# Attention inputs packed into one array, and its products as 64 by 64 tiles

## The chip, the core and the metric

The kernel runs on one core of one Trainium2 chip. The metric is the device time of one execution in microseconds (us); the lower the better. Each core has five engines with a queue of instructions each: PE (TensorE, matrix products), DVE (VectorE), ACT (ScalarE), POOL (GpSimd) and SP (SyncE), whose queue here issues nearly all of the transfers (DMAs) between memory and the core. Engines wait for one another, and for transfers, through semaphores.

## What is computed

The reference chains three layers over 4608 tokens of width 512:

```python
# 1: attention within chunks of 64 tokens, 8 heads of 64
scores = scale * np.matmul(q_c, k_c.transpose(0, 1, 2, 4, 3))
scores = scores - np.max(scores, axis=-1, keepdims=True)
attn = np.exp(scores)
attn = attn / (np.sum(attn, axis=-1, keepdims=True) + 1e-09)
out = np.matmul(attn, v_c)
# 2: a mixture of 8 experts, each token to its best one, or to none where x @ w_skip <= 0
h = np.maximum(xc[mask] @ w1[e], 0.0)
y[mask] = gate_w[mask, None] * (h @ w2[e])
# 3: a gated linear unit
g = x @ w_gate
silu = g * (1.0 / (1.0 + np.exp(-g)))
return (silu * (x @ w_val) @ w_out)
```

Only the first layer's input and its two products (scores, and attention times values) are touched by the change; everything is float32 there.

## The kernel before

The program has three stages: attention with the routing of tokens to experts, the experts, and the gated linear unit. The order of the instructions on each engine is written out by hand. The change lies in the first stage.

**Tiles.** The attention stage loops over 36 tiles `i` of 128 tokens, that is of two chunks of 64 tokens with 8 heads. Heads are held in pairs: partitions 0 to 63 hold the first head of each of four pairs, partitions 64 to 127 the second. A step of the loop does, in this order: `qk(i)` (scores of tile i on PE into the PSUM tile `s`), `pv(i-2)` (values, PE into `o`), for one tile in four a piece of the routing, `sums(i-1)` (DVE), `ta(i-1)` (four transposes on PE into `at`, copied to `ats` by ACT), `tx(i-4)` (the store of a finished tile `x` to the array X in memory, four transposes into `xp`, a copy by ACT), then `soft(i)` (DVE: the maximum `mx`, and `a`, scores minus maximum), `norm(i-2)` (DVE: `x`, `o` divided by the sums) and `expo(i)` (ACT). Small DVE instructions of the routing are threaded in between, one after each DVE step (`link`).

**Routing.** For each group of four tiles there are `route_a` (PE products `lp`, copied by ACT), `route_b` (PE transposes `lt`, then a chain of small DVE steps that begins with `L`), and `route_c` (small PE products `rp`, more DVE steps up to `slots`). When `slots` of a group is there, POOL scatters the group's tokens into the table `perm` by four indirect DMAs (L707).

**Inputs.** Queries, keys and values are three arrays in memory. One load serves a group `g` of two tiles (256 tokens): `load_qk` issues the queries of 512 KB over 128 partitions (L498), and the keys in two DMAs of 256 KB, each over 64 partitions (L501); `load_v` does the same with the values (L506). Keys and values go into zero-padded buffers, `kbd` and `vbd`, three of each: the first head's half stands in the columns of `h2` = 0 with zeros in the other partitions, the second head's half in those of `h2` = 1. So one product of 128 rows, 64 columns of the array and 128 streamed columns (2 heads by 64) gives both heads of a pair for one chunk: eight for `qk`, eight for `pv`. The profile has two matmul records for each float32 product, 16 for each call. From tile 3 on, every odd tile issues the load of the group that lies two after its own.

**Weights.** From tile 16 on each step also splits a slice of an expert's weights (`pump`): a DMA of 512 KB into `st` for every second tile, ACT and POOL work on it.

PSUM has eight banks: `s` two buffers of one bank, `o` two buffers of one bank, `at`, `xp`, `lp` and the routing's `m` one bank each.

The functions that the change touches, with the line numbers of the profile:

Of the kernel before, what the change touches and what calls it, by code (L numbers as in the profile page):

```python
# [31 lines left out]
NG = NT // GT  # L32
NTILE = NT // P
RT = 4
# [15 lines left out]
def attention_moe_glu_kernel(  # L50
    ctx: ExitStack,
    tc: tile.TileContext,
    qT: bass.AP,
    kT: bass.AP,
    vg: bass.AP,
# [229 lines left out]
    # the first 256 tokens are among the first 256 of their experts: no further tile holds one  # L285
# [146 lines left out]
    ctx.enter_context(tc.manual_schedule())  # L432
    with ExitStack() as actx:
        lctx = ExitStack()
        ld = lctx.enter_context(tc.tile_pool(name="ld", bufs=1, side="right"))
        ldq = actx.enter_context(tc.tile_pool(name="ldq", bufs=3))
# [3 lines left out]
        ps_s = actx.enter_context(tc.tile_pool(name="ps_s", bufs=2, space=PSUM))  # L440
        ps_a = actx.enter_context(tc.tile_pool(name="ps_a", bufs=1, space=PSUM))
        ps_m = actx.enter_context(tc.tile_pool(name="ps_m", bufs=1, space=PSUM))

# [8 lines left out]
        # the tensor engine's clock rises with work: keep it busy while it has to wait  # L452
# [15 lines left out]
        # the first unit of the first expert takes tokens of the first groups only  # L468
# [10 lines left out]
        NB = 3  # L479
        kbd = [ld.tile([P, 2, HP, GT], F32, name=f"kbd{i}") for i in range(NB)]  # L480
        vbd = [ld.tile([P, 2, GT // CH, HP, D], F32, name=f"vbd{i}") for i in range(NB)]
        for i in range(NB):
            nc.gpsimd.memset(kbd[i][0:64, 1], 0.0)
            nc.gpsimd.memset(kbd[i][64:128, 0], 0.0)
            nc.gpsimd.memset(vbd[i][0:64, 1], 0.0)
            nc.gpsimd.memset(vbd[i][64:128, 0], 0.0)
# [5 lines left out]
        def load_qk(g, parts=1):  # L492
            t = ldq.tile([P, HP, GT], F32, tag="q", name="q")
            q_t[g] = t
            n = GT // parts
            for o in range(parts):
                sl = slice(o * n, (o + 1) * n)
                nc.sync.dma_start(out=t[:, :, sl], in_=qT[:, g, :, sl])  # L498
                for h2 in range(2):
                    r = slice(64 * h2, 64 * h2 + 64)  # L500
                    nc.sync.dma_start(out=kbd[g % NB][r, h2, :, sl], in_=kT[r, g, :, sl])  # L501

        def load_v(g):
            for h2 in range(2):
                r = slice(64 * h2, 64 * h2 + 64)
                nc.sync.dma_start(out=vbd[g % NB][r, h2], in_=vg[r, g])  # L506
# [30 lines left out]
        def qk(i):  # L537
            g, o = divmod(i, 2)
            s = ps_s.tile([P, H, CH], F32, tag="s", name="s")
# [9 lines left out]
            s_t[i] = s  # L549

        def soft(i):
            s = s_t.pop(i)
            mx = sp.tile([P, H], F32, tag="mx", name="mx")
# [588 lines left out]
```

## Time and profile before

| | |
|---|---|
| median of 3 runs | 1407.55 us (1405.59 to 1407.98) |
| span of the profiled execution, first to last instruction | 1403.8 us |
| attention loop: first score product to last `a` | 5.73 to 168.94 us |
| first product of the experts (`hp`) | 180.14 us |
| PE busy over the span | 1334.5 us (95%) |
| DVE, ACT, POOL busy | 711.4, 451.3, 287.1 us |

The profiled execution has its span alone, no time of its own as the runs have it: the median of the runs is 3.75 us longer than the span. Times in the rows are microseconds from the first instruction. PE busy is high in all stages, also where PE waits between products for little at a time, so the stage is read from the waits and from the steps of the loop.

### The profile page before, as it was taken

The page shows a single profiled execution, that of the slowest core. Times are in us where ns is not written, and L with a number is a line of the kernel's source. Part 1 is how long each engine was busy: PE and PEld are TensorE (multiplying, and loading weights), DVE is VectorE, ACT ScalarE, POOL GpSimd, SP SyncE. Part 2 cuts the span into 40 slices and gives each one's busy share as a digit, 9 for nine tenths or more (in the row PEclk, how much of TensorE's full clock was granted, in tenths as well). Part 3 has the DMA queues.
Part 4 walks back from the last instruction along what each step waited for, and adds up shares of the span by engine and source line. Part 5 has one row for each costly group of instructions (what it writes and reads, how often), then busy time and mean ns, then how long its engine had stood idle before and what let it go on. Part 6 is the DMA issues. An engine that isn't in the chain of part 4 may idle for free.

```text
span 1403.8 us, 21388 instructions
## 1 busy us (share of the span) xinstructions
PE 1334.5 (95%) x8357; PEld 1209.5 (86%) x8357; DVE 711.4 (51%) x1301; ACT 451.3 (32%) x891; POOL 287.1 (20%) x245
## 2 busy tenths in 40 slices
PE   7877889998999999999999999999999999999998
PEld 6766678887788788899999999999999999999998
DVE  6856757888887788533232333333233333232322
ACT  2434535666665533312121221212121122121221
POOL 3134544564655366300000000000000000000000
PEclk9989999999999999999999999999999999999999
DMA  9999847887787744110202020100101020201000
GB/s 231 274 247 265 225 134 231 264 298 263 266 298 244 232 152 151 35 38 1 46 0 46 1 46 0 39 8 28 18 5 42 0 46 0 46 1 39 0 23 16
DMA packets 136713, 150.86 MB, mean 107 GB/s; under 512 B 79744, under 2 KB 82304, under 8 KB 136610
## 3 DMA queue, kind: packets, MB, share of 16 engines
q1 hardware_dynamic: 131778, 138.82, 34.7%
q0 software_dynamic: 4832, 10.65, 2.2%
q8 instruction: 66, 1.08, 0.3%
q14 instruction: 37, 0.30, 0.1%
HBM read 125.61 MB, written 25.28 MB: 107 GB/s over the span
## 4 chain that ended last, share of the span: by engine, by line
PE 72%; DMA 13%; DVE 6%; issue 4%; ACT 2%; POOL 2%; SPq 0%; another core or an unknown queue 0%; ACTq 0%; POOLq 0%; DVEq 0%
DMA kbd<-in_kT_dram 8%; PE o L250 7%; PE o L249 7%; PE o L248 7%; PE pg L250 6%; PE pg L248 6%; PE pg L249 6%; PE pv L248 6%; PE pv L250 6%; PE pv L249 6%; DVE wlo L148 2%; DMA st<-in_moe_w_dram 2%; DMA perm<-pair,slots 2%; PE y L250 2%; PE hp L249 1%
## 5 line engine op out<-in xcount | busy, mean ns | idle before, releaser
L1081 DVE TENSOR_TENSOR sg<-pg,sg 128x384 f32<-128x384 f32 (+1 forms) x132 | 72.1, 546 | 326.7 <-ACT sg L1080 326.7
L1085 ACT ACTIVATE uh<-sg 128x384 fp32r<-128x384 f32 (+1 forms) x156 | 78.1, 501 | 312.0 <-DVE sg L1082 312.0
L250 PE MATMUL pg<-xh,glo 128*128 128x384 f32 (+1 forms) x528 | 175.5, 332 | 0.0
L248 PE MATMUL pg<-xh,ghi 128*128 128x384 f32 (+1 forms) x528 | 175.1, 332 | 0.0
L249 PE MATMUL pg<-xl,ghi 128*128 128x384 f32 (+1 forms) x528 | 174.8, 331 | 0.0
L248 PE MATMUL pv<-xh,ghi 128*128 128x384 f32 (+1 forms) x528 | 173.9, 329 | 0.0
L249 PE MATMUL pv<-xl,ghi 128*128 128x384 f32 (+1 forms) x528 | 173.9, 329 | 0.0
L250 PE MATMUL pv<-xh,glo 128*128 128x384 f32 (+1 forms) x528 | 173.9, 329 | 0.0
L250 PE MATMUL o<-ghi,ul 128*128 128x512 f32 x432 | 171.1, 396 | 2.2 <-POOL ul L1087 2.2
L248 PE MATMUL o<-ghi,uh 128*128 128x512 f32 x432 | 168.7, 391 | 2.6 <-ACT uh L1085 2.6
L249 PE MATMUL o<-glo,uh 128*128 128x512 f32 x432 | 170.6, 395 | 0.0
L1080 ACT ACTIVATE sg<-pg 128x384 f32<-128x384 f32 (+1 forms) x132 | 63.6, 482 | 312.6 <-PE pg L250 312.6
L148 DVE TENSOR_TENSOR wlo<-st,whi 128x512 fp32r<-128x512 f32 x165 | 145.0, 913 | 14.5 <-ACT whi L146 13.2
L146 ACT ACTIVATE whi<-st 128x512 fp32r<-128x512 f32 x240 | 138.2, 625 | 34.6 <-DMA st<-in_moe_w_dram 30.9
L1082 DVE TENSOR_TENSOR sg<-pv,sg 128x384 f32<-128x384 f32 (+1 forms) x132 | 72.1, 546 | 118.6 <-PE pv L250 118.5
L148 POOL TENSOR_TENSOR wlo<-st,whi 128x512 fp32r<-128x512 f32 x75 | 101.4, 1353 | 127.6 <-ACT whi L146 116.9
L1087 DVE TENSOR_TENSOR ul<-sg,uh 128x384 fp32r<-128x384 f32 (+1 forms) x132 | 72.2, 547 | 76.8 <-ACT uh L1085 76.8
L248 PEld LDWEIGHTS pg<-xh,ghi 128*128 128x128 f32 x528 | 99.4, 188 | 5.9
L249 PEld LDWEIGHTS pg<-xl,ghi 128*128 128x128 f32 x528 | 99.3, 188 | 5.7
L250 PEld LDWEIGHTS o<-ghi,ul 128*128 128x128 f32 x432 | 81.0, 188 | 21.7 <-POOL ul L1087 4.4
L250 PEld LDWEIGHTS pv<-xh,glo 128*128 128x128 f32 x528 | 99.3, 188 | 0.0
L249 PEld LDWEIGHTS pv<-xl,ghi 128*128 128x128 f32 x528 | 99.3, 188 | 0.0
(164 smaller groups left out, 2525.2 us busy)
## 6 DMA issues: line engine op xcount, KB each, us to landing
st<-in_moe_w_dram SPq DMA_DIRECT2D x120, 512.0 KB
vbd<-in_vg_dram SPq DMA_DIRECT2D x36, 256.0 KB
X<-x SPq DMA_DIRECT2D x36, 256.0 KB
out_dram<-os SPq DMA_DIRECT2D x36, 256.0 KB
q<-in_qT_dram SPq DMA_DIRECT2D x17, 512.0 KB
kbd<-in_kT_dram SPq DMA_DIRECT2D x34, 256.0 KB
xr<-X SPq DMA_DIRECT2D x128, 64.0 KB
gst<-in_moe_w_gate_dram SPq DMA_DIRECT2D x12, 512.0 KB
```

The source lines that it names most:

```text
L146: nc.scalar.activation(out=hi[:, k, :], in_=stage[:, k % 2, :], func=ACTF.Copy)
L148: eng.tensor_tensor(out=lo[:, k, :], in0=stage[:, k % 2, :], in1=hi[:, k, :].bitcast(F32), op=ALU.subtract)
L248: nc.tensor.matmul(ps, ah, bh, start=start, stop=False)
L249: nc.tensor.matmul(ps, ah, bl, start=False, stop=False)
L250: nc.tensor.matmul(ps, al, bh, start=False, stop=stop)
L1080: nc.scalar.activation(out=u, in_=pg, func=ACTF.Sigmoid)
L1081: nc.vector.tensor_tensor(out=u, in0=pg, in1=u, op=ALU.mult)
L1082: nc.vector.tensor_tensor(out=u, in0=pv_, in1=u, op=ALU.mult)
L1085: nc.scalar.activation(out=uh, in_=u, func=ACTF.Copy)
L1087: eng.tensor_tensor(out=ul, in0=u, in1=uh.bitcast(F32), op=ALU.subtract)
```

## The change

It does five things.

- The three arrays become one, `qkv`, in which each partition holds for each tile the queries, keys and values one after the other. `load` brings two tiles (256 tokens) with one DMA of 1536 KB over 128 partitions, 12 KB in a row in each; the first two tiles come in three DMAs. There are four buffers (`NB`), and tile i issues the load of tiles i+5 and i+6.
- `kbd`, `vbd`, their zero fills on POOL and the two DMAs by halves are gone.
- `qk` and `pv` become sixteen products each, of 64 rows by 64 columns by 64 streamed columns. A product of the first head of a pair uses partitions 0 to 63, one of the second head 64 to 127.
- The two heads' results go to different PSUM banks, so `s` and `o` take two banks each and have one buffer each. DVE reads `s` and `o`, and writes `a` and `x`, with the heads in that order (`by_half`).
- `tx` always uses the one buffer `xp`; before, the last four tiles had used the buffers of `s`. After the loop the four banks go to a pool `ps_u`. A tile of its own, `x0`, replaces a query buffer that the first gather of the experts had used.

```diff
+        def load(i, parts=1):
+            if parts == 2:
...
+                nc.sync.dma_start(out=t[:, 0, 0:2], in_=qkv[:, i, 0:2])
+                nc.sync.dma_start(out=t[:, 0, 2], in_=qkv[:, i, 2])
+                nc.sync.dma_start(out=t[:, 1], in_=qkv[:, i + 1])
+            else:
+                t = ld.tile([P, 2, 3, HP, P], F32, tag="q", name="q")
+                nc.sync.dma_start(out=t, in_=qkv[:, i:i + 2])
...
+        def quads():
             for hp in range(HP):
                 for c in range(2):
-                    t0 = o * P + c * CH
-                    nc.tensor.matmul(
-                        s[c * 64:c * 64 + 64, 2 * hp:2 * hp + 2, :],
-                        q_t[g][:, hp, t0:t0 + CH],
-                        kbd[g % NB][:, :, hp, t0:t0 + CH],
-                        start=True, stop=True,
-                    )
+                    for h2 in range(2):
+                        yield hp, slice(64 * c, 64 * c + 64), h2, slice(64 * h2, 64 * h2 + 64)
+
+        def qk(i):
+            t = q_t[i]
+            s = ps_s.tile([P, 2, 2 * HP, CH], F32, tag="s", name="s")[:, :, 0:HP, :]
+            for hp, c, h2, r in quads():
+                nc.tensor.matmul(s[c, h2, hp, :], t[r, 0, hp, c], t[r, 1, hp, c], start=True, stop=True)
             s_t[i] = s
...
+            ps = ps_s.tile([P, 2, 2 * HP, D], F32, tag="o", name="o")[:, :, 0:HP, :]
+            for n, (hp, c, h2, r) in enumerate(quads()):
+                d = (n // 2 % 2) * HP + hp
+                nc.tensor.matmul(
+                    ps[c, h2, hp, :], t[r, hp, c], v[r, 2, d // 2, (d % 2) * D:(d % 2) * D + D],
+                    start=True, stop=True,
+                )
...
-            if i < NTILE - LAG:
-                p = ps_a.tile([P, KD, P], F32, tag="xp", name="xp")
-            else:
-                p = ps_s.tile([P, KD, P], F32, tag="s", name="xp")
+            p = ps_a.tile([P, KD, P], F32, tag="xp", name="xp")
...
-            if i % 2 == 1 and 3 <= i < NTILE - 4:
-                load_qk(i // 2 + 2)
-                load_v(i // 2 + 2)
+            if i % 2 == 1 and i >= 3 and i + 2 * NB - 3 < NTILE:
+                load(i + 2 * NB - 3)
```

On SP's queue, from the first store of a tile on (L612 before, L600 after), one turn for two tiles stood so before; DMAHW is the completion of an earlier transfer, PE and DVE the engine waited for:

```order
L612 DMA X<-x 128x512 [waits DMAHW6_49,DVE_49]
L612 DMA X<-x 128x512 [waits DMAHW7_49,DVE_49]
L498 DMA q<-in_qT_dram 128x1024 [waits DMAHW0_49]
L501 DMA kbd_126<-in_kT_dram 64x1024 [waits DMAHW1_49]
L501 DMA kbd_126<-in_kT_dram 64x1024 [waits DMAHW2_49]
L506 DMA vbd_129<-in_vg_dram 64x1024 [waits DMAHW3_49,PE_49]
L506 DMA vbd_129<-in_vg_dram 64x1024 [waits DMAHW4_49]
```

The same place after:

```order
L600 DMA X<-x 128x512 [waits DMAHW6_49,DVE_49]
L600 DMA X<-x 128x512 [waits DMAHW7_49,DVE_49]
L492 DMA q<-in_qkv_dram 128x3072 [waits DMAHW0_49,PE_49]
L600 DMA X<-x 128x512 [waits DMAHW1_49,DVE_49]
L600 DMA X<-x 128x512 [waits DMAHW2_49,DVE_49]
```

Five loads have become one, of tiles that lie two further ahead; eight transfers may be under way in either kernel, since the ninth waits for the first.

On PE, one step of the loop (tile 7) stood so before:

```order
L543 MATMUL s<-kbd_125,q 64x128 [waits DVE_49]
L543 MATMUL s<-kbd_125,q 64x128 x7
L587 MATMUL o<-vbd_130,ats 64x128 [waits DVE_49,Activation_49]
L587 MATMUL o<-vbd_130,ats 64x128 x7
L576 MATMUL at<-ident,a 128x128 [waits PE_49,Activation_49]
L576 MATMUL at<-ident,a 128x128 x3
L618 MATMUL xp<-ident,x 128x128 [waits PE_49]
L618 MATMUL xp<-ident,x 128x128 x3
```

The same step after:

```order
L535 MATMUL s<-q 64x64 [waits DVE_49,PE_49]
L535 MATMUL s<-q 64x64 x15
L577 MATMUL o<-q,ats 64x64 [waits DVE_49,Activation_49]
L577 MATMUL o<-q,ats 64x64 x15
L566 MATMUL at<-ident,a 128x128 [waits PE_49,Activation_49]
L566 MATMUL at<-ident,a 128x128 x3
L603 MATMUL xp<-ident,x 128x128 [waits PE_49]
L603 MATMUL xp<-ident,x 128x128 x3
```

The order is the same. The number of products has doubled and their streamed width has halved; with one buffer instead of two, the wait of `s` for DVE is now for `a` of the tile just before, and the wait of `o` for `x` of the tile just before.

On PE again, the end of the stage: the gathered tokens of the first expert (L301 before, L299 after) and the last two tiles' transposes, up to the first product `hp`, stood so before:

```order
L301 MATMUL xp<-ident,x_2070 128x128 [waits DMASW1_49,PE_49]
L301 MATMUL xp<-ident,x_2070 128x128 x3
L618 MATMUL xp<-ident,x 128x128 [waits DVE_49,PE_49]
L618 MATMUL xp<-ident,x 128x128 x3
L618 MATMUL xp<-ident,x 128x128 [waits DVE_49,Activation_49]
L618 MATMUL xp<-ident,x 128x128 x3
L248 MATMUL hp<-xh,whi 128x256 [waits Activation_49]
```

And after:

```order
L299 MATMUL xp<-ident,x_2491 128x128 [waits DMASW1_49]
L299 MATMUL xp<-ident,x_2491 128x128 x3
L603 MATMUL xp<-ident,x 128x128 [waits DVE_49]
L603 MATMUL xp<-ident,x 128x128 x3
L603 MATMUL xp<-ident,x 128x128 [waits Activation_49]
L603 MATMUL xp<-ident,x 128x128 x3
L246 MATMUL hp<-xh,whi 128x256
```

Nothing moved, but both L603 now write the buffer that the gathered tokens' first tile has used: the first waits for DVE's `xl` out of it, the second for ACT's copy of the first.

## Rows read from the trace of the kernel before

**Rows 1.** The page: the profiled execution.

```profile
span 1403.8 us, 21388 instructions
```

**Rows 2.** Busy time by stretch: us, engines busy (count), PEclk, DMA share, GB/s.

```profile
45.00:80.00 35.00, 30.78 (x367) 25.37 (x367) 25.50 (x79) 14.50 (x28) 7.99 (x8) 0.90 1.06 264
115.00:150.00 35.00, 29.26 (x352) 24.00 (x348) 23.84 (x67) 17.05 (x34) 16.38 (x15) 0.93 1.04 267
280.00:320.00 40.00, 37.43 (x218) 32.11 (x217) 34.83 (x49) 25.45 (x50) 23.30 (x18) 1.00 0.85 285
```

**Rows 3.** The chain that ended last, 56 to 153: start us, us, what.

```profile
58.41 11.50 DMA kbd<-in_kT_dram
...
142.00 9.64 DMA kbd<-in_kT_dram
```

**Rows 4.** Waits, 20 to 155: us in total, times, longest us.

```profile
PE s L543 <- DMA kbd<-in_kT_dram: 13.5, 6, 3.6
...
ACT whi L146 <- DMA st<-in_moe_w_dram: 9.1, 2, 8.3
```

**Rows 5.** Timeline, DVE's `a` of tiles 0, 9, 12, 13, 29, 33, 35.

```profile
8.47 0.69 DVE L557 TENSOR_TENSOR a<-s,mx 128x512 f32<-128x512 f32 x1
...
45.74 0.68 DVE L557 TENSOR_TENSOR a<-s,mx 128x512 f32<-128x512 f32 x1
...
55.33 0.69 DVE L557 TENSOR_TENSOR a<-s,mx 128x512 f32<-128x512 f32 x1
...
60.68 0.68 DVE L557 TENSOR_TENSOR a<-s,mx 128x512 f32<-128x512 f32 x1
...
143.32 0.68 DVE L557 TENSOR_TENSOR a<-s,mx 128x512 f32<-128x512 f32 x1
...
161.84 0.68 DVE L557 TENSOR_TENSOR a<-s,mx 128x512 f32<-128x512 f32 x1
...
168.94 0.69 DVE L557 TENSOR_TENSOR a<-s,mx 128x512 f32<-128x512 f32 x1
```

**Rows 6.** Timeline, the last scatter of two groups and ACT's next `ats`.

```profile
137.37 0.97 POOL L707 DMA_INDIRECT perm<-pair,slots  x1 [0.31 <-issue]
...
139.38 0.60 ACT L578 ACTIVATE ats<-at 128x512 f32<-128x512 f32 x1 [5.97 <-PE s L543]
...
153.67 0.66 PE L576 MATMUL at<-ident,a 128*128 128x128 f32 x4
...
156.44 0.97 POOL L707 DMA_INDIRECT perm<-pair,slots  x1 [0.30 <-issue]
157.00 0.60 ACT L578 ACTIVATE ats<-at 128x512 f32<-128x512 f32 x1 [4.65 <-PE s L543]
```

**Rows 7.** Groups by line and form, 0 to 320: busy us, mean ns of one.

```profile
L543 PE MATMUL s<-kbd,q 128*64 128x128 f32 x576 | 45.0, 303 | 21.7 <-DMA kbd<-in_kT_dram 16.0 <-DVE rs L568 2.0 <-DVE slots L697 1.6
...
L618 PE MATMUL xp<-ident,x 128*128 128x128 f32 x144 | 22.9, 284 | 2.5 <-DVE d L653 2.5
...
L682 PE MATMUL rp<-oh,ones 128*128 128x8 bf16 x9 | 1.5, 166 | 0.0
```

**Rows 8.** Timeline, products on PE: start us, us from the first to the last end.

```profile
40.53 0.60 PE L618 MATMUL xp<-ident,x 128*128 128x128 f32 x4
...
42.05 1.09 PE L543 MATMUL s<-kbd,q 128*64 128x128 f32 x16
...
65.34 0.24 PE L682 MATMUL rp<-oh,ones 128*128 128x32 bf16 x4
```

**Rows 9.** Timeline, the first loads' issue and the first scores.

```profile
1.32 1.42 SPq L501 DMA_DIRECT2D kbd<-in_kT_dram  x2
...
5.73 1.97 PE L543 MATMUL s<-kbd,q 128*64 128x128 f32 x16 [1.87 <-DMA kbd<-in_kT_dram]
```

**Rows 10.** Timeline, the end of the stage.

```profile
178.02 0.60 ACT L622 ACTIVATE xt<-xp 128x512 f32<-128x512 f32 x1 [3.82 <-PE xp L618]
...
180.14 0.38 PE L248 MATMUL hp<-xh,whi 128*128 128x256 f32 x1
```

More of the change, by code (lines that the diff above doesn't have):

```diff
@@ L31 @@
 GT = 256
-NG = NT // GT
 NTILE = NT // P
+NB = 4
 RT = 4
@@ L490, in attention_moe_glu_kernel @@
         q_t = {}
[L492 to L506, printed above, removed]
+        def load(i, parts=1):
[5 more added lines that the diff above has]
+            else:
+                t = ld.tile([P, 2, 3, HP, P], F32, tag="q", name="q")
+                nc.sync.dma_start(out=t, in_=qkv[:, i:i + 2])
+            for n in range(2):
+                q_t[i + n] = t[:, n]
         wg = xtp.tile([P, KD, 32], F32, name="wg")
@@ L557, in soft @@
             nc.vector.tensor_tensor(
-                out=a, in0=s, in1=mx.unsqueeze(2).to_broadcast([P, H, CH]), op=ALU.subtract
+                out=by_half(a), in0=s, in1=mx.unsqueeze(3).to_broadcast([P, 2, HP, CH]), op=ALU.subtract
             )
@@ L581, in pv @@
         def pv(i):
-            g, o = divmod(i, 2)
+            v = q_t.pop(i)
             t = at_t.pop(i)
-            ps = ps_a.tile([P, H, D], F32, tag="o", name="o", bufs=2)
-            for hp in range(HP):
-                for c in range(2):
-                    nc.tensor.matmul(
-                        ps[c * 64:c * 64 + 64, 2 * hp:2 * hp + 2, :],
-                        t[:, hp, c * 64:c * 64 + 64],
-                        vbd[g % NB][:, :, 2 * o + c, hp, :],
-                        start=True, stop=True,
-                    )
+            ps = ps_s.tile([P, 2, 2 * HP, D], F32, tag="o", name="o")[:, :, 0:HP, :]
[5 more added lines that the diff above has]
+                )
             o_t[i] = ps
@@ L603, in norm @@
             nc.vector.tensor_tensor(
-                out=x, in0=ps, in1=rs.unsqueeze(2).to_broadcast([P, H, D]), op=ALU.mult
+                out=by_half(x), in0=ps, in1=by_half(rs.unsqueeze(2).to_broadcast([P, H, D])), op=ALU.mult
             )
@@ L718, in attention_moe_glu_kernel @@
         warm_up(24, ps_a, "lp")
-        load_qk(0, 2)
-        load_qk(1)
-        load_v(0)
-        load_v(1)
-        load_qk(2)
-        load_v(2)
+        load(0, 2)
+        for i in range(2, 2 * NB, 2):
+            load(i)
         pending = []
@@ L752, in attention_moe_glu_kernel @@
             if i == NTILE - 4:
-                xs = ldq.tile([P, 2, DM], F32, tag="q", name="x0")
+                xs = x0p.tile([P, 2, DM], F32, name="x0")
                 nc.gpsimd.memset(xs, 0.0)
@@ L1113, in qk_layout @@
     def qk_layout(a):
-        a = a.reshape(8, HP, 2, 576, D).transpose(2, 4, 1, 0, 3).reshape(P, HP, NG, GT)
-        return np.ascontiguousarray(a.transpose(0, 2, 1, 3))
-    v = inputs["v"].reshape(8, HP, 2, 9, CH, D).transpose(2, 4, 0, 3, 1, 5)
-    v = np.ascontiguousarray(v.reshape(P, NG, GT // CH, HP, D))
-    out = {"qT": qk_layout(inputs["q"]), "kT": qk_layout(inputs["k"]), "vg": v}
-    for n in _INS[3:]:
+        return a.reshape(8, HP, 2, 576, D).transpose(2, 4, 0, 3, 1).reshape(P, NTILE, P, HP).transpose(0, 1, 3, 2)
+    v = inputs["v"].reshape(8, HP, 2, 9, CH, D).transpose(2, 4, 0, 3, 1, 5).reshape(P, NTILE, HP, P)
+    out = {"qkv": np.ascontiguousarray(np.stack([qk_layout(inputs["q"]), qk_layout(inputs["k"]), v], axis=2))}
+    for n in _INS[1:]:
         a = np.ascontiguousarray(inputs[n])
```

36 lines of the change are left out of this document (14 added, 22 removed).

## The prediction

> **What bounds the kernel now.** Only the attention stage is touched, 180 of the 1403.8 us of the profiled execution [rows 1, 10]; what comes behind it starts from its end and should move with it. I read that stage in four steps.
>
> First the table by stretch [rows 2]. From 45 to 150 us the DMA engines are busy all the time (shares of 1.06 and 1.04, over 1 since packets overlap) and move 264 to 267 GB/s. DVE, the busiest of the computing engines beside PE, is busy for 25.50 of 35 us. In a stretch of the experts, where all loads are 128 partitions wide, a share of 0.85 moves 285 GB/s, which is 335 at a full share. So transfers are the limit in the loop, and it moves bytes more slowly than this chip does elsewhere.
>
> Then the chain [rows 3]. From 58.41 to 151.64 us it consists of nine links, all of them transfers: the first and the last stand there, keys both; each ends when a transfer lands that lets SP issue the next. The waits say the same with smaller numbers [rows 4]: PE waited 13.5 us for keys, ACT 9.1 us for weights that were late in the same queue.
>
> Last the steps of the loop, from one `a` to the next [rows 5], to see what is left without transfers. Tiles 9 to 12 wait for no load: 9.59 us for three steps, 3.2 us each. The step to tile 13, one with a routing chain, took 5.35, so four steps make 14.94. But the last four before tile 33 took 18.52, though no load held DVE there. The reason is another wait [rows 6]: ACT's `ats` of tile 31 starts at 157.00, though PE had the transposes ready at 153.67 + 0.66 = 154.33. Near by, POOL had begun the last of its four scatters at 156.44. In the group before, `ats` starts at 139.38, 1.04 us after the last scatter ended (137.37 + 0.97). So a run of scatters costs 18.52 - 14.94 = 3.6 us in one step of four, and the change leaves the scatters as they are.
>
> **The change part by part.**
>
> *One load for 256 tokens.* Two tiles need 1.573 MB of inputs and 0.524 MB of stores, from tile 16 on also 0.524 MB of weights: 2.10, later 2.62 MB. At 265 GB/s that is 7.9 and 9.9 us, against 2 x 3.2 = 6.4 to 7.5 us of computing without scatters and 9.3 us with them (half of 14.94 and 18.52): the transfers lose everywhere. If loads of 128 partitions run at the 335 GB/s of the experts, it is 6.3 and 7.8 us: they keep up everywhere, narrowly so at first. No row shows 12 KB runs over 128 partitions, so I bound the rate by 265 below and by 335, its nearest row, above, and take 335: the keys' and values' halves are what the attention stage has and the experts' has not. Two tiles more of lead (four buffers) cover the rest.
>
> What this gives, tile by tile. The first scores begin at 5.73, which is 2.99 us after the last of three issues ended at 2.74 [rows 9]. Now they wait for one DMA, issued from about 0.8 on for 0.7 us (half of 1.42): 4.5 us. [...] From scores to `a` it was 8.47 - 5.73 = 2.74, and with one buffer the next scores wait for `a` to end: 2.74 + 0.69 + 0.1 = 3.5 us a step for three steps. So `a` of tile 0 at 7.2, of tile 3 at 17.7. Five steps of 3.2 to tile 8 and one of 5.35 give tile 9 at 39.1, where it was at 45.74: 6.7 us earlier. From 9 to 13 nothing changes (14.94). From tile 13 to tile 33 it took 161.84 - 60.68 = 101.2 us; five cycles of 18.52 are 92.6: 8.6 us earlier. The last two steps keep their 7.1. **Sum for the loop: 15.3 us.**
>
> *The zero fills and the spared issues.* POOL's fills lie ahead of its first scatter, and SP has time between issues: nothing. Their cover is that POOL has no other work there; without it one fill more or less would move only the first keys, which came later by their DMA [rows 9].
>
> *Products of 64 by 64.* The records show how PE takes small products. Transposes of 128 columns, one after the other, step by (0.60 - 0.284) / 3 = 105 ns; the 16 records of a score call step by (1.09 - 0.303) / 15 = 52 ns, half of that, since two products in different 64-column halves of the array run together [rows 7, 8]. A call now has 32 records of half the width. If all four quarters run together, it is 32 x 13 = 0.42 us of stepping; if only the two column halves do, 32 x 26 = 0.83, the same as now; if none do, 32 x 52 = 1.68. The smallest step that a row shows is (0.24 - 0.166) / 3 = 25 ns between loads of weights with tiny products, and 32 x 25 = 0.8 us. I take 0.8: scores and values cost what they cost now, and the loop gets nothing from them, since DVE, not PE, sets the 3.2 us. The lower bound of 0.4 would take less than 1 us from the step with a routing chain: nine times, at most 8 us in all; the upper one is a rival.
>
> [...]
>
> *One buffer instead of two for `s` and `o`.* PE's scores of tile i now wait for `a` of i-1, and behind them stand on PE `pv`, `at`, `xp`. Between the end of one `a` and the next `mx` DVE has `x` and the sums to do, about 0.2 + 0.2 + 0.7 + 0.6 = 1.7 us by its steps; scores need 1.09. So 0.6 us are left: nothing. If a routing product (1.0 us) stands ahead of them, that cover is gone, and ACT's wait for the same product hides it, as it does now. Bound: 0.4 us for nine steps, 4 us. DVE's reads of two banks have the same 512 elements in each partition: nothing.
>
> *One buffer `xp` at the end.* ACT copies tile 33 out of it only at 178.02 [rows 10]; the gathered tile must wait for that, and tile 34 for DVE to read the gathered one. That puts two copies of 0.60 and a read of 0.7 in a row that used to overlap, ahead of `hp` (180.14). I take 2.0 us later; bounds 0 and 3.
>
> **Sum:** -15.3 + 2.0 = -13.3 us, or 1403.8 - 13.3 = 1390.5 us for the span, and 1407.55 - 13.3 = **1394.2 us** for the median, which lies 3.75 us above the span.
>
> **The rivals.**
>
> *A. The scatters' wait goes too.* If it is long only because transfers crowd the queues, the five cycles take 14.94 instead of 18.52 us: 17.9 us more, 1376.3 us. For it: tile 13, the first with scatters, cost only 5.35. Against it: the wait ends about 1 us behind the last scatter in both groups of [rows 6].
>
> *B. The loads are no faster.* If 12 KB runs move at the old 265 GB/s, the loop goes at 7.9 and 9.9 us for two tiles as now; only the start is won (1.2 us) and the end is lost (2.0): 1408.4 us, no change. For it: no row has such loads. Against it: the 335 GB/s of the experts. [...]
>
> *C. PE becomes the bound: slower.* If no two quarters run together, a call's 32 records step by 52 ns: 1.68 us, with 0.1 between calls. A tile takes PE 2 x 1.78 + 0.5 (`at`) + 0.43 (`xp`) and a fourth of the routing's 2 us: 5.0 us. 35 steps make 175, `a` of tile 35 comes at 182 instead of 168.94: 13.3 us later, with the end 1423 us. It decides from (168.94 - 7.2) / 35 = 4.6 us a tile on. Against it: column halves do run together today.
>
> *D. The clock falls.* PE has less to do in each step. In [rows 2] it is granted 0.90 and 0.93 where PE waits for loads, 1.00 in the experts. [...] Against it: without waits for loads no gap of PE is as long as the 3.6 us of [rows 4].
>
> **How the numbers follow.** Forecast 0.60, A 0.17, B 0.10, C 0.08, D 0.05. The forecast's own range comes from its bounds: -8 for quick products, -3 for a start at the full clock, +4 for single buffers, +1 at the end: 1384 to 1400. For 8 in 10 I leave out C and half of A and of D, so from 1373 (A with a part of the quicker start) to 1410. A measurement of this kernel can tell about 0.2%, 2.8 us, from no change. Faster: the forecast, A and a little of B, 0.78; same: most of B and the forecast's edge, 0.09; slower: C, D and the rest, 0.13.
>
> **What would show it.** No wait of PE for the loads after tile 2, and a chain without transfers from 58 to 151; a DMA share clearly under 1 in the loop; steps of 3.2 us without and over 5 with a routing chain; a score call of about 1 us; cycles of 18.5 us with scatters (A: 15); `hp` at about 167. I am wrong if the share stays at 1 with 265 GB/s (B), a call takes over 1.7 us (C), or PEclk falls below 0.9 (D).

## The result and the profile after

| | before | after |
|---|---|---|
| median | 1407.76 us, 4 runs | 1423.89 us (1417.41 to 1427.16), 4 runs |
| ratio to before | | 1.0106, 95% interval 1.0079 to 1.0132 |
| profiled execution, span | 1403.8 us | 1421.3 us |
| last `a` of the loop | 168.94 us | 176.23 us |
| first product of the experts (`hp`) | 180.14 us | 193.78 us |
| from `hp` to the end | 1223.7 us | 1227.5 us |

The change made the kernel 1.1% slower; 1394.2 us was forecast. Most of it, 13.6 us, is there when the experts begin. Over the kernels below whose experts get the reference's rows, the stretch from `hp` to the end varies from 1223.5 to 1228.0 us, so I don't explain its 3.8 us. Every number read from a trace, here and below, is of one execution. The totals of one kernel's executions lie 3 to 18 us apart (9.8 us for after), so a few us between two traces tell nothing.

The transfers did what the forecast said. The table by stretch of the kernel after, in the columns of [rows 2]:

```profile
45.00:80.00 35.00, 25.43 (x530) 19.89 (x530) 23.75 (x75) 11.72 (x23) 7.67 (x8) 0.84 0.77 231
115.00:150.00 35.00, 26.86 (x486) 21.17 (x485) 20.88 (x61) 15.60 (x30) 15.82 (x15) 0.77 0.77 244
```

The DMA share is 0.77 where it was over 1: the loads are no longer the limit. But DVE is busy for less of each stretch than in [rows 2], so fewer tiles go through, and PE is granted 0.84 and 0.77. The waits from 20 to 155 us (total us, times, longest) say what took the place of the 13.5 us for keys in [rows 4]:

```profile
PE s L535 <- issue: 13.5, 16, 1.7
...
ACT ats L568 <- remote: 8.5, 2, 4.5
PE o L577 <- issue: 7.3, 10, 2.2
...
DVE mx L544 <- remote: 3.6, 2, 2.2
PE lp L615 <- issue: 2.6, 1, 2.6
```

No load is among them. "issue" is a wait for nothing that the profile shows, "remote" one for a signal that comes from nowhere it knows. DVE's `a` of tiles 9, 12, 13, 28, 29, 33 and 35 in the timeline answers to [rows 5]:

```profile
45.54 0.68 DVE L547 TENSOR_TENSOR a<-s,mx 128x512 f32<-128x512 f32 x1
...
55.54 0.69 DVE L547 TENSOR_TENSOR a<-s,mx 128x512 f32<-128x512 f32 x1
...
63.83 0.68 DVE L547 TENSOR_TENSOR a<-s,mx 128x512 f32<-128x512 f32 x1
...
139.64 0.69 DVE L547 TENSOR_TENSOR a<-s,mx 128x512 f32<-128x512 f32 x1
...
149.19 0.68 DVE L547 TENSOR_TENSOR a<-s,mx 128x512 f32<-128x512 f32 x1
...
169.00 0.68 DVE L547 TENSOR_TENSOR a<-s,mx 128x512 f32<-128x512 f32 x1
...
176.23 0.68 DVE L547 TENSOR_TENSOR a<-s,mx 128x512 f32<-128x512 f32 x1
```

The loop starts early (`a` of tile 0 at 6.13 us), and at tile 9 all of the lead is gone. Plain steps are nearly as before, 10.0 us for three from 9 to 12. The step to tile 29, the one in which a group's scatters run, took 9.55 us for 7.74 before. Two places show the two new waits. First, tile 7's scores on PE:

```profile
29.10 0.65 PE L535 MATMUL s<-q 64*64 64x64 f32 x26 [0.42 <-DVE rs L586]
...
31.43 0.38 PE L535 MATMUL s<-q 64*64 64x64 f32 x4 [1.69 <-issue]
```

PE stops in the midst of one call, between two products that need the same data. Up to the end of this gap and of four others (at 17.9, 40.55, 71.97 and 115.15 us), the table by stretch counts PE's matmuls and weight loads, the second and third numbers in brackets:

```profile
0.00:17.88 17.88, 10.60 (x220) 9.11 (x220) 9.86 (x25) 4.14 (x6) 2.29 (x15) 0.71 0.90 353
0.00:31.42 31.42, 20.48 (x470) 17.36 (x471) 20.27 (x46) 10.07 (x17) 2.29 (x15) 0.78 0.89 332
0.00:40.54 40.54, 26.95 (x595) 22.16 (x596) 25.57 (x57) 12.87 (x22) 2.29 (x15) 0.79 0.87 320
0.00:71.96 71.96, 50.07 (x1097) 40.60 (x1098) 46.30 (x119) 24.99 (x45) 6.37 (x19) 0.81 0.80 269
0.00:115.14 115.14, 83.71 (x1725) 65.98 (x1726) 73.32 (x197) 43.53 (x80) 22.99 (x34) 0.79 0.82 264
```

The sums are 440, 941, 1191, 2195 and 3451. The differences, 501, 250, 1004 and 1256, are two, one, four and five times 250 or 251. The page of after says what comes in such pieces:

```profile
PE 1338.1 (94%) x9509; PEld 1207.1 (85%) x9509; DVE 714.4 (50%) x1301; ACT 451.4 (32%) x891; POOL 275.4 (19%) x233
...
q8 instruction: 75, 1.23, 0.4%
```

The page of before:

```profile
PE 1334.5 (95%) x8357; PEld 1209.5 (86%) x8357; DVE 711.4 (51%) x1301; ACT 451.3 (32%) x891; POOL 287.1 (20%) x245
...
q8 instruction: 66, 1.08, 0.3%
```

The queue of instructions has 75 packets of 16.4 KB for 2 x 9509 matmuls and weight loads of PE, 254 to a packet; before it had 66 for 2 x 8357. The 9 packets more for 2304 instructions more are 256 each. The transfers of after show when: two, one, four and five of these packets begin between one of the five places and the next, and the last one ahead of each, at 15.5, 29.2, 37.3, 69.8 and 112.8 us, begins 2.2 to 3.2 us before PE goes on. PE stops where one packet's worth ends, and goes on after the next has come: **its instructions come late.**

Not every wait put down to "issue" is of this kind. The scores that stand behind a routing step's transposes `lt` wait too, seven times in the loop, at tiles 10, 14 and every fourth after:

```profile
46.32 0.69 PE L535 MATMUL s<-q 64*64 64x64 f32 x32 [1.04 <-issue]
...
129.52 1.13 PE L535 MATMUL s<-q 64*64 64x64 f32 x32 [1.04 <-issue]
```

Each time they begin 0.10 us after DVE's `a` of the tile before has ended (the first `a` above ends at 45.54 + 0.68 = 46.22): they wait for the one buffer `s`. PE's 32 waits for "issue" from 10 to 175 us are therefore of three kinds: 8 at the end of a packet (10.7 us), these 7 for `a` (7.7 us), and 17 while scatters run (9.0 us), which come next.

Second, the scatters ahead of tile 25 (SP and the weight loads left out):

```profile
118.22 0.99 POOL L692 DMA_INDIRECT perm<-pair,slots  x1 [2.93 <-DVE slots L682]
...
118.64 0.66 PE L566 MATMUL at<-ident,a 128*128 128x128 f32 x4
...
120.66 0.75 PE L535 MATMUL s<-q 64*64 64x64 f32 x14
...
121.80 0.36 PE L535 MATMUL s<-q 64*64 64x64 f32 x4 [0.39 <-issue]
...
122.11 0.98 POOL L692 DMA_INDIRECT perm<-pair,slots  x1 [0.30 <-issue]
122.53 0.37 PE L535 MATMUL s<-q 64*64 64x64 f32 x4 [0.37 <-issue]
122.62 0.60 ACT L568 ACTIVATE ats<-at 128x512 f32<-128x512 f32 x1 [3.97 <-remote]
...
123.97 0.57 PE L535 MATMUL s<-q 64*64 64x64 f32 x9 [1.07 <-issue]
...
124.34 0.31 PE L535 MATMUL s<-q 64*64 64x64 f32 x1
...
125.66 1.12 PE L566 MATMUL at<-ident,a 128*128 128x128 f32 x4 [0.15 <-issue]
...
126.56 1.06 PE L603 MATMUL xp<-ident,x 128*128 128x128 f32 x4
```

While POOL scatters, from 118.2 to 123.1, the scores trickle, four records at a time, and take from 120.66 to 124.65, where a call takes 0.69 us at a granted clock of 1.00 and 1.13 us at 0.50 (the two lines at 46.32 and 129.52). ACT's `ats` waits until 122.62 for transposes that ended at 118.64 + 0.66 = 119.30. Then `at` and `xp` run at a granted clock of 0.50, 1.1 us each for 0.6 to 0.66.

### The profile page after: what moved, and what is told of

The parts are those of the page before. It is cut to its first block, busy times and chain, and to the rows that moved or that the text cites. A ratio compares the mean times of both kernels' runs of the same rounds, so it can differ in the third digit from the quotient of the medians.

```text
span 1421.3 us, 23581 instructions
## 1 busy us (share of the span) xinstructions
PE 1338.1 (94%) x9509; PEld 1207.1 (85%) x9509; DVE 714.4 (50%) x1301; ACT 451.4 (32%) x891; POOL 275.4 (19%) x233
## 4 chain that ended last, share of the span: by engine, by line
PE 75%; DVE 9%; issue 5%; DMA 5%; ACT 3%; POOL 2%; another core or an unknown queue 1%; SPq 0%; POOLq 0%; ACTq 0%; DVEq 0%
PE o L248 7%; PE o L247 7%; PE o L246 7%; PE pg L248 6%; PE pg L246 6%; PE pg L247 6%; PE pv L246 6%; PE pv L248 6%; PE pv L247 6%; DVE wlo L146 3%; DMA st<-in_moe_w_dram 2%; DMA perm<-pair,slots 2%; PE y L248 2%; PE y L247 1%; PE hp L246 1%
## 5 line engine op out<-in xcount | busy, mean ns | idle before, releaser
L146 DVE TENSOR_TENSOR wlo<-st,whi 128x512 fp32r<-128x512 f32 x165 | 153.0, 962 | 13.6 <-ACT whi L144 11.7
L1065 DVE TENSOR_TENSOR sg<-pv,sg 128x384 f32<-128x384 f32 (+1 forms) x132 | 72.1, 546 | 118.2 <-PE pv L248 118.0
L246 PEld LDWEIGHTS pv<-xh,ghi 128*128 128x128 f32 x528 | 99.3, 188 | 0.0
```

Source lines behind the costliest of these rows:

```text
L146: eng.tensor_tensor(out=lo[:, k, :], in0=stage[:, k % 2, :], in1=hi[:, k, :].bitcast(F32), op=ALU.subtract)
L246: nc.tensor.matmul(ps, ah, bh, start=start, stop=False)
L1065: nc.vector.tensor_tensor(out=u, in0=pv_, in1=u, op=ALU.mult)
```

## Experiments

The theories: **I**, PE's instructions come late; **C**, the low clock; **B**, one buffer of `s` and `o`; **S**, scatters hold up PE's signals, the more of them the longer. (Their letters are not those of the rivals: theory C is rival D.) Ratios are to the kernel before, run beside each; after stands at 1.0106. "Last a", "hp" and the mean step to tiles 21, 25, 29 and 33 (those behind the scatters) are from the timelines, the clock and the DMA share from 17.7 to 150 us.

| run | ratio (95%) | last a | hp | steps | clock | share |
|---|---|---|---|---|---|---|
| before | 1 | 168.94 | 180.14 | 7.41 | 0.91 | 1.03 |
| after | 1.0106 (1.0079-1.0132) | 176.23 | 193.78 | 9.04 | 0.80 | 0.80 |
| x4_dense16 | 0.9893 (0.9851-0.9936) | 153.50 | 167.75 | 6.01 | 0.99 | 0.89 |
| x5_wide32 | 0.9997 (0.9976-1.0019) | 171.37 | 183.15 | 5.69 | 0.91 | 0.85 |
| x6_thin16 | (1.0830) | 199.16 | 212.46 | 8.23 | 0.62 | 0.67 |
| x3_old32 | 1.0040 (1.0018-1.0063) | 175.38 | 189.41 | 7.75 | 0.95 | 1.02 |
| x2_twobuf | 0.9991 (0.9967-1.0015) | 161.96 | 177.32 | 7.50 | 0.90 | 0.86 |
| x1_load4k | 1.0054 (1.0033-1.0076) | 174.03 | 190.21 | 8.70 | 0.86 | 0.84 |
| x11_load1 | 1.0008 (0.9975-1.0040) | 169.15 | 179.55 | 5.61 | 0.85 | 0.91 |
| x7_spread_after | 1.0044 (1.0022-1.0067) | 174.29 | 186.92 | 6.78 | 0.82 | 0.87 |
| x8_spread_before | 1.0005 (0.9982-1.0028) | 172.86 | 181.31 | 5.78 | 0.88 | 1.03 |
| x12_two_spread | 0.9934 (0.9906-0.9963) | 159.57 | 171.37 | 6.74 | 0.87 | 0.94 |
| y4_two_spread_load1 | 0.9933 (0.9908-0.9958) | 151.59 | 163.86 | 5.97 | 0.94 | 0.91 |
| y1_noscat_after | (0.9933) | 158.10 | 169.79 | 5.19 | 0.88 | 0.78 |
| z2_noscat_dense16 | one run | 149.52 | 161.07 | 5.31 | 0.99 | 0.81 |
| y2_fill_after | 1.0372 (1.0337-1.0407) | 211.08 | 223.10 | 6.63 | 0.92 | 0.66 |
| x9_inter | 0.9942 (0.9914-0.9971) | 162.40 | 170.73 | 5.64 | 0.90 | 0.99 |
| x10_inter_spread | 0.9952 (0.9926-0.9978) | 158.83 | 167.32 | 5.88 | 0.96 | 1.01 |
| y3_inter_early | 0.9960 (0.9935-0.9986) | 159.32 | 167.23 | 5.11 | 0.96 | 1.00 |
| z1_inter_start | 0.9865 (0.9839-0.9890) | 148.09 | 157.33 | 5.62 | 0.95 | 0.97 |

Ratios in brackets are of kernels whose experts get other rows than the reference's; only their loop is read.

**Number, size and clock of the products.** x4_dense16 (values likewise, here and in the next two):

```diff
             for hp, c, h2, r in quads():
-                nc.tensor.matmul(s[c, h2, hp, :], t[r, 0, hp, c], t[r, 1, hp, c], start=True, stop=True)
...
+                if c.start == 0:
+                    nc.tensor.matmul(s[:, h2, hp, :], t[r, 0, hp, :], t[r, 1, hp, :], start=True, stop=True)
...
```

> The changed kernel with 16 records a call: each product of 64 rows takes both chunks' 128 columns and 128 streamed columns, so that the second chunk's scores and values are those of other pairs (only the time is of interest). Theories I and S: instructions are as many as before, no stalls put down to 'issue', cycles of four tiles fall from 20.4 to 18.5 us or less, the time to 1395 to 1410. Theory C: PE is no busier and the clock no better, 1418 to 1426. Theory B: no change, 1424.

1394.56 us, the forecast's 1394.2. The last `a` at 153.50 is the forecast's 168.94 - 15.3 = 153.64, with one buffer of `s` and of `o` and the packed loads. So what the forecast said of loads and buffers holds in its total as long as a call has 16 records. Each of these records streams twice the columns, and the clock is 0.99: x4 differs from after in more than the number. (Half of its scores are of other pairs, so its tokens are routed otherwise; from `hp` to the end it takes 1224.4 us, within the range above.) The scatters ahead of its tile 25 in the timeline:

```profile
121.22 1.00 POOL L690 DMA_INDIRECT perm<-pair,slots  x1 [2.41 <-DVE slots L680]
122.11 0.66 PE L567 MATMUL at<-ident,a 128*128 128x128 f32 x4
...
123.34 0.60 ACT L569 ACTIVATE ats<-at 128x512 f32<-128x512 f32 x1 [1.70 <-PE xp L601]
...
124.13 1.16 PE L536 MATMUL s<-q 64*128 64x128 f32 x16
125.09 0.97 POOL L690 DMA_INDIRECT perm<-pair,slots  x1 [0.30 <-issue]
```

`ats` starts 0.57 us after its transposes end, in the middle of the scatters, and the scores run through them. x5_wide32 keeps after's number of records and doubles the columns that each streams:

```diff
-                nc.tensor.matmul(s[c, h2, hp, :], t[r, 0, hp, c], t[r, 1, hp, c], start=True, stop=True)
...
+                o = (HP + hp) * P + c.start
+                nc.tensor.matmul(s[c, h2, hp, :], t[r, 0, hp, c], f[r, o:o + P], start=True, stop=True)
```

> The changed kernel with 128 columns streamed in each product in place of 64 (the second 64 fall into the halves of the banks that are not used), so that PE has as many records as after, each twice as long. Theory C (what costs is the low clock that light work brings): PEclk rises to 0.95 or more and the time falls to 1395 to 1410. Theories I, S and B (what costs is the number of records, or that they can't run ahead): 1420 or more, at whatever clock.

Between the two: 15 us better than after, 14 worse than x4, at a clock of 0.91. Its steps behind scatters are short (5.69 us); PE's waits for "issue" from 10 to 175 us, summed over its lines, stay at 25.4 us (27.4 in after, 2.5 before). None of them falls into a scatter any more (the table of waits below). x6_thin16 halves x4's streamed columns:

```diff
-                    nc.tensor.matmul(s[:, h2, hp, :], t[r, 0, hp, :], t[r, 1, hp, :], start=True, stop=True)
+                    nc.tensor.matmul(s[:, h2, hp, :], t[r, 0, hp, :], t[r, 1, hp, c], start=True, stop=True)
```

> The changed kernel with one product for both chunks' columns and 64 streamed columns: half of the records, each no longer than after (the second chunk's scores and values are those against the first chunk's keys and values; only the time is of interest). Theories I and S (the number of records costs): 1390 to 1400 as with the 16 longer records, though PEclk is as low as after. Theory C: the clock stays at 0.8 and the time above 1412.

Against every theory but C: half of the work of x4, in as many records, takes 46 us more in the loop, at a mean clock of 0.62. By stretch:

```profile
17.70:45.00 27.30, 27.30 (x206) 25.06 (x204) 15.73 (x32) 7.97 (x14) 0.00 (x0) 0.50 0.66 205
45.00:80.00 35.00, 33.63 (x253) 28.08 (x251) 16.89 (x48) 11.08 (x20) 4.06 (x4) 0.56 0.48 158
```

PE is busy for all of the first stretch, at a granted clock of 0.50, and for 33.63 of the 35 us of the second, at 0.56. Its routing fills one expert, so the loop over further tiles adds some 90 us behind `hp`; its total says nothing. x3_old32 cuts before's products in two and leaves all else:

```diff
+                    for h2 in range(2):
+                        nc.tensor.matmul(
+                            s[c * 64:c * 64 + 64, 2 * hp + h2, :],
+                            q_t[g][:, hp, t0:t0 + CH],
+                            kbd[g % NB][:, h2, hp, t0:t0 + CH],
...
```

> The kernel before with each zero-padded product of 128 streamed columns cut into two of 64, so that a call has 32 records as after, with the loads, buffers and order of before. Theory S: the steps behind the scatters grow from 7.5 to about 9.5 us, 14 us in seven cycles, 1420. Theory I with the count of instructions as its cause: stalls put down to 'issue' appear, 5 to 15 us, 1413 to 1422; with the long transfers as its cause: none, 1408 to 1411. Theory C and B: no change, 1407 to 1411.

5.6 us slower than before at a clock of 0.95, with "issue" waits of 14.9 us: the number of records costs without the packed array, without the low clock and with two buffers.

**Buffers.** x2_twobuf gives `s` and `o` the two halves of their banks in turn:

```diff
+        s_all = ps_s.tile([P, 2, 2, HP, CH], F32, tag="s", name="s")
...
-            s = ps_s.tile([P, 2, 2 * HP, CH], F32, tag="s", name="s")[:, :, 0:HP, :]
+            s = s_all[:, :, i % 2]
```

> The changed kernel with two buffers of s and of o again, as the two halves of the same four banks. Theory B: PE runs ahead by a tile again, steps behind the scatters fall from 9.5 us to about 8, and the time falls by 5 to 10 us, to 1414 to 1419. Theories I and S: the wait only moves, within 3 us of 1424.

15 us, more than B expected, and "issue" waits fall to 11.5 us; 7.7 of the 15.9 us less are the waits for `a`, which are gone. x4 has one buffer of each and meets the forecast, so with 16 records no such cost shows (no run has 16 records, the packed array and two buffers). That two buffers give PE a lead in which a stop passes unseen is argued, not shown.

**Transfers and instructions.** x1_load4k makes the load three transfers with 4 KB runs, x11_load1 makes it one for each tile:

```diff
-                nc.sync.dma_start(out=t, in_=qkv[:, i:i + 2])
+                for n in range(3):
+                    nc.sync.dma_start(out=t[:, n], in_=qkv[:, i // 2, n])
```

```diff
...
-            if i % 2 == 1 and i >= 3 and i + 2 * NB - 3 < NTILE:
-                load(i + 2 * NB - 3)
+            if i >= 2 and i + 2 * NB - 2 < NTILE:
+                load(i + 2 * NB - 2)
```

> The packed array with its pairs of tiles as three transfers (queries, keys, values; 4 KB in a row in each of 128 partitions) in place of one with 12 KB; nothing else changes. Theory I (PE runs out of instructions: its stream has twice the products, its blocks of 16 KB come through the same DMA engines and come late behind the long transfers): PE's waits put down to 'issue' between 10 and 175 us fall from 27 us to under 10, and the time falls by 8 us or more, to 1415 or less. Theory C (the low clock), theory B (one buffer of s and o) and theory S (scatters hold back PE's signals, and more products wait on them): nothing of theirs changes, 1421 to 1426.

> The changed kernel with one load of 768 KB a tile (6 KB in a row) in place of one of 1536 KB for two. Theory I (blocks of instructions come late; long loads ahead of them make it worse): the stalls at each 256th instruction of PE shrink and the time falls by 3 to 8 us, to 1416 to 1421. The others: 1421 to 1426.

Both are faster, by 7 and 14 us, and neither by I's reason: "issue" waits stay at 27.1 and 28.8 us. The steps behind scatters fall in x11 to 5.61 us, but the loop gains nothing by it from tile 13 to 33 (104.2 us, 105.2 in after): other steps grow, the one to tile 15 to 12.0 us, as PE stands at the end of a packet (at the sum of 2195 again):

```profile
71.12 0.80 PE L573 MATMUL o<-q,ats 64*64 64x64 f32 x18 [7.91 <-issue]
```

Of the 14.2 us that x11 wins up to `hp`, 6.3 are there at tile 13, and 7.1 come behind the last `a`. That long loads make instructions late is not borne out.

**Scatters.** x7_spread_after and x8_spread_before:

```diff
-            while pending and (i % 4 == 3 or i >= NTILE - LAG):
+            for _ in range(len(pending) if i >= NTILE - LAG else min(1, len(pending))):
                 scatter(pending.pop(0))
```

> The changed kernel with the four scatters of a group issued one in each step in place of four in a row. Theory S (PE's signals pile up while scatters run, and more records pile up more): a single scatter holds back less than PE's next wait, so that the steps of 9.5 us behind the scatters fall to about 6 and the time by 10 to 20 us, to 1404 to 1414. Theories I, B and C: within 4 us of 1424.

> The kernel before with the four scatters of a group one in each step. Theory S: the steps behind the scatters fall from 7.5 to about 6, but the transfers still set the pace of the loop, so 1400 to 1408. The others: 1406 to 1411.

After gains 9 us, though its "issue" waits grow to 34.6 us; before, with its loads as the limit, nothing. The steps behind the scatters fall to 6.78 us, yet from tile 13 to 33 the loop takes 104.0 us, after 105.2: 4.9 of the 6.9 us won up to `hp` come behind the last `a`. PE's stops in x7 stand where they stood in after, at sums of 2195 and 3451, though 1.2 us apart in time at the second:

```profile
0.00:72.10 72.10, 48.24 (x1097) 39.14 (x1098) 46.25 (x119) 25.10 (x45) 6.35 (x19) 0.90 0.85 269
0.00:116.31 116.31, 77.34 (x1725) 62.70 (x1726) 74.23 (x197) 43.66 (x80) 23.08 (x34) 0.85 0.87 260
```

y1_noscat_after and z2_noscat_dense16 replace the loop's scatters by `pending.clear()`.

> The changed kernel with the scatters of the loop left out (the table of rows stays empty for all but the last groups, so the experts work on the dummy row; only the attention loop's time is of interest). If scatters make the long steps (tiles 21, 25, 29 at 9.2 to 9.6 us), these steps fall to 6 or less and the last 'a' comes 15 us earlier or more, by 161. If the low clock and late instructions make them, they stay above 8 us, and the last 'a' comes after 168.

> The kernel with 16 records a call on the packed array (second chunk's products wrong), with the scatters of the loop left out too; only the attention loop's time is of interest. With 32 records the scatters' absence brought the last 'a' from 176.2 to 158.1 us. Theory S (scatters cost more, the more records wait on them): here it brings little, from 153.5 to 146 or later. If scatters cost the same whatever the number of records: to 136.

This is the clearest of the tables. First `hp`, us:

| | 16 records a call | 32 records a call |
|---|---|---|
| with scatters | 167.75 | 193.78 |
| without | 161.07 | 169.79 |

In this program scatters cost 6.7 us with 16 records and 24.0 us with 32. Of the 26.0 us between after and x4, 17.3 are that difference; 8.7 are there without scatters. Sorted as above (an `a` that has just ended, the count of instructions, scatters under way), PE's waits for "issue" from 10 to 175 us are, in us:

| | all | ends of packets | for `a` | scatters | other |
|---|---|---|---|---|---|
| after | 27.4 | 10.7 | 7.7 | 9.0 | 0 |
| x5_wide32 | 25.4 | 18.1 | 7.3 | 0 | 0 |
| x7_spread_after | 34.6 | 27.1 | 7.3 | 0.2 | 0 |
| x11_load1 | 28.8 | 20.5 | 8.3 | 0 | 0 |
| y1_noscat_after | 22.9 | 15.3 | 7.3 | 0 | 0.3 |
| x4_dense16 | 10.1 | 0 | 7.5 | 2.6 | 0 |
| z2_noscat_dense16 | 7.6 | 0 | 7.3 | 0 | 0.3 |

With 32 records PE stops at the ends of packets in every one of these runs, and for longer where the stops in scatters are gone. In x4 and z2 no wait goes by packets: all but the 0.3 us recur at the same places of the loop's cycle, 358 instructions apart. The seven waits for `a` are there with 16 records too:

```profile
58.01 1.16 PE L536 MATMUL s<-q 64*128 64x128 f32 x16 [1.04 <-issue]
```

The late signals don't go by the number of records. A call of scores has one signal, in before as in after (36 in all). At five tiles behind scatters up to tile 31 `ats` starts late, 0.6 to 3.5 us in before and 2.1 to 4.4 us in after; in x4 it is 0.55 to 1.04 us at six. In x5 and x11, which have 32 records and four scatters in a row, no `ats` behind a scatter is over 0.35 us late, nor any in y1 and z2. So theory S holds in that scatters make PE's signals late, not in that more records make them later; what decides it is open. x12_two_spread (x2 and x7 together) and y4_two_spread_load1 (with x11 too):

> The changed kernel with two buffers of s and o in the halves of their banks, and the scatters one in each step. Theories B and S with separate costs: 1408.8 less 5 to 11, so 1398 to 1404. If both remove the same wait, or if instructions come late whatever is done: 1405 to 1411.

> The changed kernel with two buffers of s and o, spread scatters and one load a tile. If shorter loads are worth by themselves what the run with one load a tile showed, 1388 to 1394; if they and the two buffers removed the same waits, 1395 to 1400.

Both beat both kernels, at 1396.91 and 1395.22 us. Shorter loads add nothing that can be measured in the total. With all of its 32 records y4 reaches `hp` at 163.86 us, no later than x4.

**The clock.** y2_fill_after:

```diff
...
+                for n in range(2):
+                    nc.tensor.matmul(
+                        f, ident, q_t[i][:, 0, 2 * n:2 * n + 2].rearrange("p h k -> p (h k)"), start=True, stop=True
+                    )
```

> The changed kernel with two further products of 128 rows and 256 streamed columns a step (8 more instructions, some 0.9 us of PE) into the unused half of s, behind the transposes of xp; nothing reads them. Theory C (the low clock costs): PEclk rises to 0.9 or more and the time falls by 5 us or more, to 1419 or less. Theories I, S, B: the time stays or grows by up to 10 us, 1422 to 1434.

It tells nothing of C: the clock rises to 0.92, but every plain step takes 5.3 us for 3.2. The filler writes the same tile `s`, so DVE's `mx` waits for it, 2.0 to 2.2 us a step; the next scores wait for `a`, and the next filler stands behind them, the values, `at` and `xp`.

**The loads alone.** x9_inter keeps before's products, buffers and number of loads; the two heads of a pair lie in the even and the odd partitions, so that a half of 64 partitions spans the whole width:

```diff
...
-                    r = slice(64 * h2, 64 * h2 + 64)
+                    r = slice(h2, P, 2)
                     nc.sync.dma_start(out=kbd[g % NB][r, h2, :, sl], in_=kT[r, g, :, sl])
```

> The kernel before with the two heads of a pair interleaved over the partitions (the first head in the even ones, the second in the odd ones), so that each half of the keys and values, still zero-padded and still 64 partitions, is loaded over the whole width; products, records, buffers and the number of loads stay. It is the forecast's first term alone. If that term was right, the loop keeps up with its loads and the time falls by 8 to 15 us, to 1393 to 1400. If halves were not what made the loads slow, nothing changes, 1406 to 1411.

x10_inter_spread adds x7's edit, y3_inter_early issues two loads of weights at tile 13:

> The same with the scatters one in each step in place of four in a row. Theory S for 16 records: the steps behind the scatters are at 6 us already when loads are quick, so a further 0 to 5 us, 1390 to 1400; if scatters one by one hold back more steps, 1 to 5 us slower than without.

> The interleaved kernel with 16 records a call and spread scatters, and the first two loads of the experts' weights issued at tile 13 in place of 16: ACT's wait of 5.4 us for them is gone, tile 18's step falls from 10.4 to 5 us, the time to 1391 to 1396. If the wait only moves to the keys, 1397 to 1401.

All three gain 6 to 8 us, and the two edits add nothing that can be told. (The step of 10.4 us in the last expectation was misread: tile 18 took 8.08 us in x10 and 6.58 in y3.) But the first `a` came at 20.5 us. The zero fills, now of whole tiles, held the first keys back (in y3 they are issued at 14.10 us, in before at 1.32). z1_inter_start, with all of these edits, moves them:

```diff
+        nc.vector.memset(kbd[0], 0.0)
...
+            nc.scalar.activation(out=f, in_=zcol.to_broadcast([P, 2 * HP * GT]), func=ACTF.Copy)
```

> The interleaved kernel with spread scatters and early weights, and its zero fills moved off the start (the first by VectorE ahead of all else, three by ScalarE, two left on GpSimd): in the run before the first 'a' came at 20.5 us for 8.5 in the kernel before, and the loop from there took 139 us for 160.5. If the start is all that hid the loads' gain, the first 'a' comes by 11 us and the time falls by 8 to 11 us, to 1386 to 1391; if the loop then waits for its first loads instead, 1392 to 1398.

**1385.20 us (1382.29 to 1388.50), ratio 0.9865 (0.9839 to 0.9890):** the best of all, 2.4% below after. By stretch:

```profile
45.00:80.00 35.00, 30.66 (x370) 25.70 (x370) 27.52 (x84) 16.61 (x31) 11.43 (x11) 0.90 0.98 260
115.00:150.00 35.00, 30.27 (x378) 25.36 (x377) 30.68 (x81) 19.73 (x38) 18.87 (x17) 0.96 0.92 259
```

Its rates in these two stretches are no higher than in [rows 2], but it had moved more ahead of them: from 17.7 to 150 us it moves 286 GB/s, x9 302, before 259. From the first `a` to the last it takes 138.2 us, before 160.5. x9, without the scatters' and the weights' edits, takes 141.7 us, so the loads are worth some 19 of these 22 us. They still set the pace, with a share of 0.97 and this wait of PE from 20 to 140 us:

```profile
PE s L552 <- DMA kbd<-in_kT_dram: 12.0, 6, 3.9
```

## Why the prediction was wrong

**The step that failed** is the one on products of 64 by 64: "I take 0.8: scores and values cost what they cost now, and the loop gets nothing from them". The duration was fine, even too long: a call takes 0.69 us at a granted clock of 1.00, and of the prediction's three estimates only that of all four quarters together, 0.42 us, lies below it. What I left out is that a call had become 64 instructions. I priced the products by PE's time, and PE was not the limit. With 16 records, each of twice the columns, the same program takes the forecast's time (x4); after takes 26.0 us more up to `hp`, 17.3 of them through the scatters (y1, z2) and 8.7 without them. That the number alone costs is shown by x3: 5.6 us at a clock of 0.95, with the old loads and two buffers. Without scatters PE stops at the ends of packets for 15.3 us with 32 records and not at all with 16. That these stops are all of the 8.7 us is argued, not shown: the clock differs too, 0.88 (y1) and 0.99 (z2). The nearest to a run with 32 records and its instructions in time is y4, with two buffers, single scatters and shorter loads: 6.8 us at the ends of packets, a clock of 0.94, and `hp` no later than in x4.

**The loads** were right in mechanism: a share of 0.80 from 17.7 to 150 us in after, 1.03 in before, and no wait of PE for them after tile 2. The size, 153.50 for 153.64 us in x4, is in part luck: x4's `a` of tile 13 comes at 57.3 us, 3.2 later than the forecast's 39.1 + 14.94 = 54.0, and its five cycles take 88.6 us, 4.0 less than the forecast's 92.6. x9 and z1 show by another edit that loads over the whole width are faster: 302 and 286 GB/s from 17.7 to 150 us, before 259. No run shows the 3 us that the range takes for a start at the full clock: the first call of before takes 1.97 us at a granted clock of 1.00 (5.73 to 7.70), a later one 1.09 us, also at 1.00 (42.05).

**One buffer** was put at nothing with a bound of 4 us. That holds with 16 records; with 32 it is 15 us (x2). My 0.6 us of cover was counted on a PE that never stops. The seven waits for `a`, 1.04 us each, cost nothing that shows: the step from tile 13 to 14 takes 3.23 us in before, after and x4.

**The scatters** were to stay at 18.52 us a cycle "as they are"; they took 20.45 (tiles 25 to 29; 21.0 in the mean from tile 13 to 33). I read [rows 6] as late signals alone, with PE running on; in after PE itself stops in the midst of its calls.

**One `xp` at the end:** 2.0 us forecast; from the last `a` to `hp` x4 takes 14.2 us, 3.0 more than before, the upper bound. That the buffer `xp` makes it isn't shown: x5, x11, y1 and z2, which have the same one buffer, take 10.4 to 11.8 us. After takes 17.5; while its last scatters run, `ats` waits for 6.35 us:

```profile
183.62 0.69 DVE L591 TENSOR_TENSOR x<-o,rs 128x512 f32<-128x512 f32 x1 [4.23 <-remote]
...
185.15 0.60 ACT L568 ACTIVATE ats<-at 128x512 f32<-128x512 f32 x1 [6.35 <-remote]
...
193.78 0.56 PE L246 MATMUL hp<-xh,whi 128*128 128x256 f32 x1
```

**The rivals.** Rival C's 1423 us is the time that came, by another way: a call takes 0.69 us, 22 ns a record, or 1.13 at a granted clock of 0.50, more only where PE stops, and PE is busy for 25 to 27 of 35 us. Rival D was right that PEclk falls below 0.9, to 0.77; the values, `at`, `xp` and `lt` took 0.4 to 0.5 us longer each ahead of tile 25, 1.8 us together. How much of the 26 us is the clock's stays open: x5 raises clock and work together, and y2 puts other work on the path. Rival A fell with 32 records; with 16 a part of it is there, 17.16 us a cycle in x4 (tiles 25 to 29). Rival B is out: the loads are faster, from 17.7 to 150 us 247 GB/s at a share of 0.80 in after, 259 at 1.03 in before. (The range's bounds add up to 1383.2 and 1399.2 us, not 1384 and 1400; nothing hangs on it.)

## What to carry to other kernels

Count instructions, not only the time of the array: here smaller tiles cost the array nothing (a call took 0.69 us for 1.09) and left PE waiting at the ends of packets for 10.7 us. Before a wait for "issue" is taken for a late instruction, look whether a neighbour has just ended: seven of after's 32 were waits for DVE. Before a buffer is given up because there is slack, ask for the longest stop of the engine that fills it: the second buffers were worth 15 us here (x2). Where a transfer by halves is slow, let the halves interleave over the partitions before changing the products that need them (302 GB/s for 259 here, x9).

## What the runs showed of the hardware

- PE's instructions come in packets of 16.4 KB: 9 more of them for 2304 instructions more, 256 each. At 64 a call, PE stopped at their ends for up to 2.6 us in after and 7.9 us in x11; at 32 a call (x4, z2) no wait goes by packets.
- While POOL's scatters run four in a row, PE's signals come up to 4.4 us late in after's loop, and PE stops in the midst of a call. Leaving the scatters out gains 24.0 us with 32 records a call (y1), 6.7 with 16 (z2). With shorter loads (x11) or wider products (x5) neither is seen; by which path it works is open.
- From 17.70 to 45 us PE was busy for all of 27.3 us in x6 and was granted 0.50; in x4, with twice the streamed columns in as many records, it was busy for 24.7 us and was granted 1.00.
- Halves of 64 partitions that span the whole width move 302 to 317 GB/s in the loop (x9, 45 to 80 and 115 to 150 us), for 264 to 267 in [rows 2]; from 17.7 to 150 us 302 for 259.
- While POOL filled whole tiles, from 1.99 to 10.76 us, a copy of 8 columns on DVE took 9.09 us (y3), 1.11 us in before.
